# Attention feeding an expert layer: q, k and v loaded as 72 partitions, first batch cast by the DMA, x in token order

## The chip, the cores and the metric

One core of a Trainium2 chip runs the whole program. The metric is device time in microseconds (us). The engines are PE (matrix multiply; PEld is its weight load), VectorE (DVE in the profile), ScalarE (ACT), GpSimd (POOL) and SyncE (SP). DMAs are issued from SP's queue or from POOL's; those that convert fp32 to bf16 on the way are issued from POOL.

## The reference

Eight batches of eight heads; 576 tokens and a head size of 64. Keys and values are averaged over groups of eight tokens, so that 72 remain. Then comes an expert layer with h times cos(h) in the middle.

```python
k_p = k.reshape(B, H, Sp, pool, D).mean(axis=3)      # pool 8, Sp 72
v_p = v.reshape(B, H, Sp, pool, D).mean(axis=3)
scores = scale * np.matmul(q, k_p.transpose(0, 1, 3, 2))
attn = np.exp(scores); attn = attn / np.sum(attn, axis=-1, keepdims=True)
attn_out = np.matmul(attn, v_p)
x = attn_out.transpose(0, 2, 1, 3).reshape(B * S, H * D)   # 4608 x 512
h = x @ w_in                                               # 4608 x 2048
out = (h * np.cos(h)) @ w_out                              # 4608 x 512
```

## The kernel before

The 4608 tokens are nine tiles of 512. For each tile t the loop runs an **up** pass and a **down** pass. Up (`up`, L284 to L289) multiplies 64 times 128x512 on PE into three double PSUM banks in turn; ScalarE takes the cosine (a sine with a bias, L288), VectorE multiplies it with h into `g_sb` (L289). Down (`down_mm`, L292) multiplies 64 times more: four slices `ms` of 128 tokens, 16 steps each, into two single PSUM banks `obanks`. VectorE copies a finished slice to SBUF (L297) and SP stores it.

The attention of batch b = t + 1 is put between the down matmuls of tile t. The list `fill` gives to each piece of it the slot (the number of the down matmul) ahead of which it is issued; a piece that waits holds everything behind it on its engine, since the order on each engine is that of the program. In tiles 1 to 6 the pieces are the transposes of pooled k and of q at slots 2, 6 and 10, and from slot 14 every three slots one of: `scores` (two matmuls into bank 0 and an exponential on ScalarE, L211, L214), `sums` (four matmuls with ones into bank 1, a logarithm and an exponential of its negative, L221 to L225), and `values` with `normal` (four matmuls into bank 2 and a multiply on VectorE, which writes x transposed into `xT`, L234, L243). In tile 0 the pieces start at slot 36 and the attention at slot 48, one slot apart. ScalarE loads another function table for the sine and for the exponential, twice in each tile.

**Loads.** q comes cast to bf16 from POOL's queue as `q_main` (128 partitions of four tokens, 1 KB of fp32 each) and `q_rem` (the last 64 tokens, 256 bytes each). k and v are 72 partitions of eight tokens, 2 KB of fp32 per head; each load is cut into 64 and 8 partitions (`by_rows`). Batch 0's k comes uncast from SP in two halves of four heads; v of batch 0 and k, v of batch 1 come cast from POOL; k, v of batch 2 uncast from POOL, all others uncast from SP. POOL's order at the start is q of batch 0, v of batch 0, the weights, k, q, v of batch 1, k, q, v of batch 2.

**Pooling.** Batch 0's k: VectorE adds tokens 0-3 to 4-7 (L153), PE adds the remaining four and transposes in one, by matmuls with the identity (L146). Batch 0's v and batch 1's k and v: PE adds all eight by matmuls with the identity (L146, L159). From batch 2 on, POOL adds in three steps (`pool_kv`, L121 to L123).

**Order of the columns.** q's transposes (L179, L191) give the tokens of a batch as four blocks of 128 (tokens 0, 4, 8, ... first) and one of 64 (`col_of`). The columns of `xT` keep that order, and `down_out` stores rows with a stride of four.

**Start.** Batch 0's attention stands alone ahead of the loop: halves of k and q, scores of heads 0 to 3, then the other halves, then v, then rounds of `values`, `sums` and `scores`, and the first up pass.

```python
        eng.tensor_tensor(out=s[:, :, 0:4, :], in0=s[:, :, 0:4, :], in1=s[:, :, 4:8, :], op=ADD)
        eng.tensor_tensor(out=s[:, :, 0:2, :], in0=s[:, :, 0:2, :], in1=s[:, :, 2:4, :], op=ADD)
        eng.tensor_tensor(out=dst, in0=s[:, :, 0, :], in1=s[:, :, 1, :], op=ADD)
```

Of the kernel before, what the change touches and what calls it, by code (L numbers as in the profile page):

```python
# [14 lines left out]
POOL = 8  # L15
# [4 lines left out]
def kernel(  # L20
# [27 lines left out]
    kvb = ctx.enter_context(tc.tile_pool(name="kvb", bufs=3))  # L48
    kvst = ctx.enter_context(tc.tile_pool(name="kvst", bufs=2))
    qst = ctx.enter_context(tc.tile_pool(name="qst", bufs=3))  # L50
# [15 lines left out]
    def by_rows(dst, src):  # L66

        for lo, hi in ((0, 64), (64, Sp)):
            yield dst[lo:hi], src[:, lo:hi]

    def kv_view(src, b):
        return src[b].rearrange("h (p t) d -> h p (t d)", t=POOL)

    def load_kv(b, which, src, queue=nc.sync):
        st = kvst.tile([Sp, H, POOL, D], FP32, name="kv_st", tag="kv_st")
        for o, i in by_rows(st.rearrange("p h t d -> p h (t d)"), kv_view(src, b)):
            queue.dma_start(out=o, in_=i.rearrange("h p n -> p h n"))
        staged[which, b] = st

    def load_kv_cast(b, which, src):  # L80
        st = kvb.tile([Sp, H, POOL, D], BF16, name=f"{which}_b", tag="kv_b")
        for o, i in by_rows(st.rearrange("p h t d -> p h (t d)"), kv_view(src, b)):
            nc.gpsimd.dma_start(out=o, in_=i.rearrange("h p n -> p h n"))
        staged[which, b] = st

    def load_k_halves(b):
        hs = H // 2
        for j in range(2):
            st = kvst.tile([Sp, H, POOL, D], FP32, name="kv_st", tag="kv_st")[:, 0:hs]
            for o, i in by_rows(st.rearrange("p h t d -> p h (t d)"), kv_view(k, b)[j * hs:(j + 1) * hs]):  # L90
                nc.sync.dma_start(out=o, in_=i.rearrange("h p n -> p h n"))
            staged["k", b, j] = st

    def load_q(b, halves=1):
        qm = qst.tile([128, H, 4, D], BF16, name="q_main", tag="q_main")
        qr = qst.tile([64, H, D], BF16, name="q_rem", tag="q_rem")
        hs = H // halves
        for j in range(halves):
            hh = slice(j * hs, (j + 1) * hs)
            nc.gpsimd.dma_start(out=qm[:, hh].rearrange("p h t d -> p h (t d)"),  # L100
                                in_=q[b, hh, 0:512, :].rearrange("h (p t) d -> p h (t d)", t=4))
            nc.gpsimd.dma_start(out=qr[:, hh], in_=q[b, hh, 512:S, :].rearrange("h s d -> s h d"))
        pooled["q", b] = (qm, qr)
# [22 lines left out]
    def col_of(b, t):  # L126

        if b % 2 == 0:
            return 128 * t
        return 0 if t == 4 else 64 + 128 * t  # L130

    att = {}

    def heads(x, pj):
        return x[:, 2 * pj:2 * pj + 2]

    def pool_k_mm(b, bank, kb, pjs):

        if ("kpT", b) not in att:
            att["kpT", b] = asb.tile([128, KCH, Sp], BF16, name="kpT", tag="kpT")  # L140
        n, rows = len(pjs), kb.shape[2]
        ps = bank[:, 0:n * Sp].rearrange("p (j n) -> p j n", j=n)
        for i in range(n):
            for t in range(rows):
                for hp in range(2):
                    nc.tensor.matmul(ps[hp * 64:hp * 64 + 64, i, :], lhsT=kb[:, 2 * i + hp, t, :],  # L146
                                     rhs=identity[:Sp, :Sp], start=(t == 0), stop=(t == rows - 1))
        nc.vector.tensor_copy(out=att["kpT", b][:, pjs[0]:pjs[-1] + 1, :], in_=ps)

    def pool_k_half(b, j, bank):  # L150
        st = staged.pop(("k", b, j))
        kb = asb.tile([Sp, H // 2, POOL // 2, D], BF16, name="k_sum", tag="k_sum")
        nc.vector.tensor_tensor(out=kb, in0=st[:, :, 0:4, :], in1=st[:, :, 4:8, :], op=ADD)  # L153
        pool_k_mm(b, bank, kb, range(2 * j, 2 * j + 2))
# [10 lines left out]
    def q_transpose(b, bank, pjs=range(KCH)):  # L165
# [3 lines left out]
        qT = att["qT", b]  # L169
        qb, _ = pooled["q", b]  # L170
        n = len(pjs)
        if len(bank.shape) == 3:
            bank = bank.rearrange("p a n -> p (a n)")
        ps = bank.bitcast(BF16)[:, 0:n * 512].rearrange(
            "p (j t n) -> p j t n", t=4, j=n)
        for i, pj in enumerate(pjs):
            for t in range(4):
                for hp in range(2):
                    nc.tensor.matmul(ps[hp * 64:hp * 64 + 64, i, t, :], qb[:, 2 * pj + hp, t, :],  # L179
                                     identity, is_transpose=True)  # L180
        c0 = col_of(b, 0)
        nc.vector.tensor_copy(out=qT[:, pjs[0]:pjs[-1] + 1, c0:c0 + 512],  # L182
                              in_=ps.rearrange("p j t n -> p j (t n)"))

    def q_transpose_rem(b, bank, pjs=range(KCH)):
        qT = att["qT", b]
        _, qrb = pooled["q", b]
        n = len(pjs)
        ps = bank.bitcast(BF16)[:, 0:n * 64].rearrange("p (j n) -> p j n", j=n)
        for i, pj in enumerate(pjs):  # L190
            nc.tensor.matmul(ps[:, i, :], heads(qrb, pj).rearrange("p h d -> p (h d)"),  # L191
                             identity[:64, :64], is_transpose=True)
        c0 = col_of(b, 4)
        nc.vector.tensor_copy(out=qT[:, pjs[0]:pjs[-1] + 1, c0:c0 + 64], in_=ps)
# [100 lines left out]
    def down_out(t, ms, ps):  # L295
        o = msb.tile([128, d_model], FP32, name="o_sb", tag="o_sb")
        nc.vector.tensor_copy(out=o, in_=ps)  # L297
        pair, r = divmod(t * 4 + ms, 9)
        if r == 4:
            for j in range(2):  # L300
                r0 = (2 * pair + j) * S + 512
                nc.sync.dma_start(out=out[r0:r0 + 64, :], in_=o[j * 64:j * 64 + 64, :])
        else:
            b, tt = (2 * pair, r) if r < 4 else (2 * pair + 1, r - 5)
            rows = out[b * S:b * S + 512, :].rearrange("(p t) m -> t p m", t=4)
            nc.sync.dma_start(out=rows[tt], in_=o)


    load_k_halves(0)
    load_q(0, 2)  # L310
    identity = consts.tile([128, 128], BF16, name="identity")
    make_identity(nc, identity)
    ones = consts.tile([128, D], BF16, name="ones")
# [3 lines left out]

# [5 lines left out]
    load_kv_cast(1, "k", k)  # L323
    load_q(1)
    load_kv_cast(1, "v", v)
    load_kv(2, "k", k, nc.gpsimd)
    load_q(2)
    load_kv(2, "v", v, nc.gpsimd)
    exp_tables()
    pool_k_half(0, 0, obanks[0])  # L330
    q_transpose(0, banks[2], range(0, 2))
    q_transpose_rem(0, banks[2][:, 1, :], range(0, 2))
    scores(0, 0, 0, banks[0])
    scores(0, 1, 0, banks[1])
    pool_k_half(0, 1, obanks[1])
    q_transpose(0, obanks[0], range(2, 4))
    q_transpose_rem(0, obanks[1], range(2, 4))
    sums(0, 0, 0, banks[2])
    scores(0, 0, 1, banks[0])
    scores(0, 1, 1, banks[1])  # L340
    pool_v_mm(0, obanks[1])
    todo = [(0, 0), (0, 1), (1, 0), (1, 1)]
    for n, (j, sg) in enumerate(todo):
        values(0, j, sg, obanks)
        normal(0, j, sg, obanks)
        if n + 1 < 4:
            sums(0, *todo[n + 1], banks[2])
        if n + 2 < 4:
# [77 lines left out]
```

The softmax here doesn't subtract the row's maximum and nothing guards it: scores larger than these inputs give would overflow.

## Time and profile before

| what | us |
|---|---|
| median of three runs (350.87 to 352.19) | 350.93 |
| the profiled execution | 351.02 |
| its span, first to last instruction | 349.2 |
| PE busy | 326.5 |
| ACT busy | 181.6 |
| DVE busy | 154.3 |
| POOL busy | 124.4 |

The page splits the span into 40 slices of 8.73 us and gives each engine's busy share in tenths. A timeline line reads: start, duration, engine, line, operation, output <- input, partitions x elements and type, count, and in brackets the idle time before it with what ended it. A line of the chain of waits reads: start, duration, engine, tile, line; the chain is followed back from the last instruction to what released it. A line of the busy times by stretch has the stretch, its length, then for PE, PEld, DVE, ACT and POOL the busy time with the number of instructions, then the clock granted to PE, the DMA share and the GB/s that the DMAs moved.

### The profile page before, as it was taken

The page shows a single profiled execution, that of the slowest core. Times are in us where ns is not written, and L with a number is a line of the kernel's source. Part 1 is how long each engine was busy: PE and PEld are TensorE (multiplying, and loading weights), DVE is VectorE, ACT ScalarE, POOL GpSimd, SP SyncE. Part 2 cuts the span into 40 slices and gives each one's busy share as a digit, 9 for nine tenths or more (in the row PEclk, how much of TensorE's full clock was granted, in tenths as well). Part 3 has the DMA queues.
Part 4 walks back from the last instruction along what each step waited for, and adds up shares of the span by engine and source line. Part 5 has one row for each costly group of instructions (what it writes and reads, how often), then busy time and mean ns, then how long its engine had stood idle before and what let it go on. Part 6 is the DMA issues. An engine that isn't in the chain of part 4 may idle for free.

```text
span 349.2 us, 4752 instructions
## 1 busy us (share of the span) xinstructions
PE 326.5 (93%) x1960; PEld 136.4 (39%) x1960; DVE 154.3 (44%) x175; ACT 181.6 (52%) x216; POOL 124.4 (36%) x80
## 2 busy tenths in 40 slices
PE   0578999889999999999999999999999999999995
PEld 0323444334433443344334433443345334444442
DVE  1421653237523762366245723572257325723731
ACT  1146640676556655665656566565666456602600
POOL 7342317750990099008920892069100000000000
PEclk9999999999999999999999999999999999999999
DMA  9999999259518941795268617770200010012011
GB/s 140 164 204 206 189 190 224 71 64 218 96 54 138 185 80 60 116 177 107 62 98 185 118 60 99 166 137 31 60 33 0 32 60 30 2 60 60 3 54 66
DMA packets 31414, 35.77 MB, mean 102 GB/s; under 512 B 5856, under 2 KB 19872, under 8 KB 31392
## 3 DMA queue, kind: packets, MB, share of 16 engines
q0 software_dynamic: 19520, 13.05, 28.4%
q1 hardware_dynamic: 11872, 22.42, 27.5%
q8 instruction: 15, 0.25, 0.3%
q14 instruction: 7, 0.06, 0.1%
HBM read 36.70 MB, written 9.44 MB: 132 GB/s over the span
## 4 chain that ended last, share of the span: by engine, by line
PE 88%; ACT 4%; DMA 4%; DVE 1%; POOL 1%; issue 1%; ACTq 0%; POOLq 0%
PE obank L292 38%; PE bank L284 36%; PE bank L211 4%; DMA v_b<-in_v_dram 4%; PE bank L221 3%; PE bank L234 3%; PE bank L179 2%; ACT inv L225 1%; ACT lnc L223 1%; ACT ex L214 1%; PE obank L159 1%; PE bank L159 0%; POOL q_main L100 0%; PE bank L191 0%; DVE qT L182 0%
## 5 line engine op out<-in xcount | busy, mean ns | idle before, releaser
L292 PE MATMUL obank<-w_out_sb,g_sb 128*128 128x512 bf16 x576 | 148.6, 381 | 0.0
L284 PE MATMUL bank<-xT,w_in_sb 128*128 128x512 bf16 x576 | 127.6, 382 | 1.4 <-DVE xT L243 0.9
L288 ACT ACTIVATE cos<-bank,half_pi 128x1024 f32<-128x1024 f32 x72 | 80.1, 1113 | 63.8 <-PE bank L284 63.8
L289 DVE TENSOR_TENSOR g_sb<-bank,cos 128x1024 bf16<-128x1024 f32 x72 | 88.2, 1225 | 52.4 <-ACT cos L288 52.4
L121 POOL TENSOR_TENSOR kv_st<-kv_st 72x2048 f32<-72x2048 f32 x12 | 54.2, 4519 | 93.1 <-DMA kv_st<-in_k_dram 91.4
L284 PEld LDWEIGHTS <-w_in_sb 128*128 128x128 bf16 x576 | 56.6, 98 | 71.0 <-issue 4.3
L214 ACT ACTIVATE ex<-bank 72x576 bf16<-72x576 f32 x64 | 40.5, 638 | 57.1 <-PE bank L211 57.1
L292 PEld LDWEIGHTS <-g_sb 128*128 128x128 bf16 x576 | 46.8, 98 | 59.6 <-issue 12.4
L243 DVE TENSOR_TENSOR xT<-bank,inv 128x576 bf16<-128x576 f32 x28 | 21.2, 758 | 67.7 <-PE bank L234 49.3
L297 DVE COPY o_sb<-obank 128x512 f32<-128x512 f32 x36 | 24.9, 691 | 41.5 <-PE obank L292 41.0
L223 ACT ACTIVATE lnc<-bank 128x576 f32<-128x576 f32 x32 | 20.8, 650 | 28.2 <-PE bank L221 27.9
L122 POOL TENSOR_TENSOR kv_st<-kv_st 72x1024 f32<-72x1024 f32 x12 | 28.2, 2347 | 0.9
L225 ACT ACTIVATE inv<-lnc 128x576 f32<-128x576 f32 x32 | 21.9, 683 | 1.0
L211 PE MATMUL bank<-qT,kpT 64*72 64x288 bf16 x128 | 20.4, 323 | 1.5 <-ACT ex L214 1.3
L211 PEld LDWEIGHTS <-kpT 64*72 64x72 bf16 x128 | 8.0, 111 | 25.1 <-issue 25.1
L221 PE MATMUL bank<-ex,ones 72*64 72x288 bf16 x128 | 15.6, 315 | 2.0 <-ACT ex L214 1.8
L234 PE MATMUL bank<-ex,vp 72*64 72x288 bf16 x112 | 12.2, 298 | 0.0
L146 PE MATMUL obank<-identity,k_sum 72*64 72x72 bf16 x32 | 1.4, 256 | 11.4 <-DVE k_sum L153 11.4
L221 PEld LDWEIGHTS <-ones 72*64 72x64 bf16 x128 | 5.5, 113 | 14.8 <-issue 14.5
L272 ACT ACT_TABLE_LOAD x8 | 10.3, 1283 | 0.9 <-PEq L410 0.7
L182 DVE COPY qT<-bank 128x2048 bf16<-128x2048 bf16 (+1 forms) x8 | 9.2, 1150 | 2.9 <-PE bank L179 2.9
L275 ACT ACT_TABLE_LOAD x8 | 10.3, 1283 | 0.1
(44 smaller groups left out, 100.1 us busy)
## 6 DMA issues: line engine op xcount, KB each, us to landing
out_dram<-o_sb SPq DMA_DIRECT2D x32, 256.0 KB, 2.3
kv_st<-in_k_dram SPq DMA_DIRECT2D x5, 1024.0 KB, 10.8
kv_st<-in_v_dram SPq DMA_DIRECT2D x5, 1024.0 KB
q_main<-in_q_dram POOLq DMA_DIRECT2D x7, 512.0 KB, 6.6
w_in_sb<-in_moe_w_in_dram POOLq DMA_DIRECT2D x4, 512.0 KB, 16.0
w_out_sb<-in_moe_w_out_dram POOLq DMA_DIRECT2D x4, 512.0 KB, 17.7
kv_st<-in_k_dram SPq DMA_DIRECT2D x2, 512.0 KB, 5.6
v_b<-in_v_dram POOLq DMA_DIRECT2D x2, 512.0 KB, 14.7
```

What stands on the lines that cost most here:

```text
L121: eng.tensor_tensor(out=s[:, :, 0:4, :], in0=s[:, :, 0:4, :], in1=s[:, :, 4:8, :], op=ADD)
L122: eng.tensor_tensor(out=s[:, :, 0:2, :], in0=s[:, :, 0:2, :], in1=s[:, :, 2:4, :], op=ADD)
L211: nc.tensor.matmul(pair[:Sp, hp, :SEG], lhsT=kpT[hp * 64:hp * 64 + 64, pj, :], rhs=qT[hp * 64:hp * 64 + 64, pj, sg * SEG:(sg + 1) * SEG])
L214: nc.scalar.activation(out=ex, in_=pair[:Sp, :, :SEG], func=ACTF.Exp, scale=scale / POOL)
L221: nc.tensor.matmul(cs[hp * 64:hp * 64 + 64, i, :SEG], lhsT=ones[:Sp, :], rhs=ex[:, hp, :])
L223: nc.scalar.activation(out=lnc, in_=cs[:, :, :SEG], func=ACTF.Ln)
L225: nc.scalar.activation(out=inv, in_=lnc, func=ACTF.Exp, scale=-1.0)
L284: nc.tensor.matmul(h[:, j, :], lhsT=w_in_sb[fc // 4][:, ki, (fc % 4) * 128:(fc % 4 + 1) * 128], rhs=xT[:, ki, t * TILE:(t + 1) * TILE], st ...
L288: nc.scalar.activation(out=cos, in_=h, func=ACTF.Sin, bias=half_pi[:, :1])
L289: nc.vector.tensor_mul(out=g_sb[:, 2 * fp:2 * fp + 2, :], in0=h, in1=cos)
L292: nc.tensor.matmul(o, lhsT=g_sb[:, fc, ms * 128:(ms + 1) * 128], rhs=w_out_sb[fc // 4][:, fc % 4, :], start=(fc == 0), stop=(fc == FFCH - 1))
L297: nc.vector.tensor_copy(out=o, in_=ps)
```

## The change

- q, k and v are all loaded as 72 partitions with eight tokens each, 2 KB of fp32 per head. Loads from POOL's queue are no longer cut into 64 and 8 partitions; loads from SP's queue still are.
- Batch 0: k, too, comes cast from POOL, in two halves that alternate with halves of q. PE adds all eight tokens of k; VectorE's addition (`k_sum`) goes.
- q is transposed in 64 matmuls of 72 columns a batch instead of 32 of 128 and 4 of 64. The copies out of PSUM reorder the columns into token order, one copy for each pair of heads, reading with a step of 72 elements. In batch 0 VectorE and ScalarE share these copies; in tiles 0 to 6 VectorE makes all four.
- x has its columns in token order; a slice of the output is one block of 128 rows.
- Eight matmuls of 512 columns over a constant tile stand first on PE. Nothing reads their result.
- The start has another order: `sums` and `scores` of the next heads ahead of v's pooling.
- Batch 1: k and v come uncast, VectorE adds them in three steps each (slots 20 and 41 of tile 0), and batch 2's loads are issued behind these. The transposes are at slots 28, 32 and 36, the attention starts at slot 38 instead of 48.

```diff
-    kvb = ctx.enter_context(tc.tile_pool(name="kvb", bufs=3))
     kvst = ctx.enter_context(tc.tile_pool(name="kvst", bufs=2))
-    qst = ctx.enter_context(tc.tile_pool(name="qst", bufs=3))
+    qst = ctx.enter_context(tc.tile_pool(name="qst", bufs=2))
...
     def load_kv(b, which, src, queue=nc.sync):
         st = kvst.tile([Sp, H, POOL, D], FP32, name="kv_st", tag="kv_st")
-        for o, i in by_rows(st.rearrange("p h t d -> p h (t d)"), kv_view(src, b)):
-            queue.dma_start(out=o, in_=i.rearrange("h p n -> p h n"))
+
+        for lo, hi in ((0, 64), (64, Sp)) if queue is nc.sync else ((0, Sp),):
+            queue.dma_start(out=st[lo:hi].rearrange("p h t d -> p h (t d)"), in_=row_view(src, b)[lo:hi])
         staged[which, b] = st
 
-    def load_kv_cast(b, which, src):
-        st = kvb.tile([Sp, H, POOL, D], BF16, name=f"{which}_b", tag="kv_b")
-        for o, i in by_rows(st.rearrange("p h t d -> p h (t d)"), kv_view(src, b)):
-            nc.gpsimd.dma_start(out=o, in_=i.rearrange("h p n -> p h n"))
+    def row_view(src, b, h0=0, h1=None):
+        return src[b, h0:h1].rearrange("h (p t) d -> p h (t d)", t=POOL)
+
+    def load_kv_cast(b, which, src, parts=1):
+        st = kvst.tile([Sp, 2 * H, POOL, D], BF16, name="kv_st", tag="kv_st")[:, 0:H]
+        load_cast(st, b, src, parts)
         staged[which, b] = st
 
-    def load_k_halves(b):
-        hs = H // 2
...
-    def load_q(b, halves=1):
-        qm = qst.tile([128, H, 4, D], BF16, name="q_main", tag="q_main")
...
-            nc.gpsimd.dma_start(out=qm[:, hh].rearrange("p h t d -> p h (t d)"),
-                                in_=q[b, hh, 0:512, :].rearrange("h (p t) d -> p h (t d)", t=4))
-            nc.gpsimd.dma_start(out=qr[:, hh], in_=q[b, hh, 512:S, :].rearrange("h s d -> s h d"))
-        pooled["q", b] = (qm, qr)
+    def load_cast(st, b, src, parts=1, only=None):
+        hs = H // parts
+        for j in range(parts) if only is None else [only]:
+            h0, h1 = j * hs, (j + 1) * hs
+            nc.gpsimd.dma_start(out=st[:, h0:h1].rearrange("p h t d -> p h (t d)"), in_=row_view(src, b, h0, h1))
+
+    def load_q(b):
+        qb = qst.tile([Sp, H, POOL, D], BF16, name="q_b", tag="q_b")
+        load_cast(qb, b, q)
+        staged["q", b] = qb
...
+    def pool_k_mm(b, bank, pjs):
+
+        kb = staged["k", b]
         if ("kpT", b) not in att:
             att["kpT", b] = asb.tile([128, KCH, Sp], BF16, name="kpT", tag="kpT")
-        n, rows = len(pjs), kb.shape[2]
+        n, rows = len(pjs), POOL
         ps = bank[:, 0:n * Sp].rearrange("p (j n) -> p j n", j=n)
         for i in range(n):
             for t in range(rows):
                 for hp in range(2):
-                    nc.tensor.matmul(ps[hp * 64:hp * 64 + 64, i, :], lhsT=kb[:, 2 * i + hp, t, :],
+                    nc.tensor.matmul(ps[hp * 64:hp * 64 + 64, i, :], lhsT=kb[:, 2 * pjs[i] + hp, t, :],
                                      rhs=identity[:Sp, :Sp], start=(t == 0), stop=(t == rows - 1))
         nc.vector.tensor_copy(out=att["kpT", b][:, pjs[0]:pjs[-1] + 1, :], in_=ps)
...
-    def pool_k_half(b, j, bank):
-        st = staged.pop(("k", b, j))
-        kb = asb.tile([Sp, H // 2, POOL // 2, D], BF16, name="k_sum", tag="k_sum")
-        nc.vector.tensor_tensor(out=kb, in0=st[:, :, 0:4, :], in1=st[:, :, 4:8, :], op=ADD)
-        pool_k_mm(b, bank, kb, range(2 * j, 2 * j + 2))
...
+    def q_transpose(b, banks_, pjs, copies):
...
+        qT, qb = att["qT", b], staged["q", b]
+        pss = [bank.bitcast(BF16)[:, 0:S].rearrange("p (t n) -> p t n", t=POOL) for bank in banks_]
+        for ps, pj in zip(pss, pjs):
+            for t in range(POOL):
                 for hp in range(2):
-                    nc.tensor.matmul(ps[hp * 64:hp * 64 + 64, i, t, :], qb[:, 2 * pj + hp, t, :],
-                                     identity, is_transpose=True)
-        c0 = col_of(b, 0)
-        nc.vector.tensor_copy(out=qT[:, pjs[0]:pjs[-1] + 1, c0:c0 + 512],
-                              in_=ps.rearrange("p j t n -> p j (t n)"))
-
-    def q_transpose_rem(b, bank, pjs=range(KCH)):
-        qT = att["qT", b]
-        _, qrb = pooled["q", b]
-        n = len(pjs)
-        ps = bank.bitcast(BF16)[:, 0:n * 64].rearrange("p (j n) -> p j n", j=n)
-        for i, pj in enumerate(pjs):
-            nc.tensor.matmul(ps[:, i, :], heads(qrb, pj).rearrange("p h d -> p (h d)"),
-                             identity[:64, :64], is_transpose=True)
-        c0 = col_of(b, 4)
-        nc.vector.tensor_copy(out=qT[:, pjs[0]:pjs[-1] + 1, c0:c0 + 64], in_=ps)
+                    nc.tensor.matmul(ps[hp * 64:hp * 64 + 64, t, :], qb[:, 2 * pj + hp, t, :],
+                                     identity[:Sp, :Sp], is_transpose=True)
+        for ps, pj, copy in zip(pss, pjs, copies):
+            copy(out=qT[:, pj, :].rearrange("p (n t) -> p n t", t=POOL), in_=ps.rearrange("p t n -> p n t"))
 
...
-        pair, r = divmod(t * 4 + ms, 9)
-        if r == 4:
-            for j in range(2):
-                r0 = (2 * pair + j) * S + 512
-                nc.sync.dma_start(out=out[r0:r0 + 64, :], in_=o[j * 64:j * 64 + 64, :])
-        else:
-            b, tt = (2 * pair, r) if r < 4 else (2 * pair + 1, r - 5)
-            rows = out[b * S:b * S + 512, :].rearrange("(p t) m -> t p m", t=4)
-            nc.sync.dma_start(out=rows[tt], in_=o)
-
-
-    load_k_halves(0)
-    load_q(0, 2)
+        r0 = t * TILE + ms * 128
+        nc.sync.dma_start(out=out[r0:r0 + 128, :], in_=o)
+
+
+    warm = consts.tile([128, 512], BF16, name="warm")
+    nc.vector.memset(warm, 1.0)
+    exp_tables()
+    k0 = kvst.tile([Sp, 2 * H, POOL, D], BF16, name="kv_st", tag="kv_st")[:, 0:H]
+    q0 = qst.tile([Sp, H, POOL, D], BF16, name="q_b", tag="q_b")
+    staged["k", 0], staged["q", 0] = k0, q0
+    load_cast(k0, 0, k, 2, 0)
+    load_cast(q0, 0, q, 2, 0)
     identity = consts.tile([128, 128], BF16, name="identity")
     make_identity(nc, identity)
+    load_cast(k0, 0, k, 2, 1)
+    load_cast(q0, 0, q, 2, 1)
     ones = consts.tile([128, D], BF16, name="ones")
     nc.gpsimd.memset(ones, float(POOL))
     half_pi = consts.tile([128, 1], FP32, name="half_pi")
     nc.gpsimd.memset(half_pi, math.pi / 2.0)
-
     load_kv_cast(0, "v", v)
     for cg in range(4):
         load_w_in(cg)
     for cg in range(4):
         load_w_out(cg)
-    load_kv_cast(1, "k", k)
+    load_kv(1, "k", k, nc.gpsimd)
     load_q(1)
-    load_kv_cast(1, "v", v)
-    load_kv(2, "k", k, nc.gpsimd)
-    load_q(2)
-    load_kv(2, "v", v, nc.gpsimd)
-    exp_tables()
-    pool_k_half(0, 0, obanks[0])
-    q_transpose(0, banks[2], range(0, 2))
-    q_transpose_rem(0, banks[2][:, 1, :], range(0, 2))
-    scores(0, 0, 0, banks[0])
-    scores(0, 1, 0, banks[1])
-    pool_k_half(0, 1, obanks[1])
-    q_transpose(0, obanks[0], range(2, 4))
-    q_transpose_rem(0, obanks[1], range(2, 4))
-    sums(0, 0, 0, banks[2])
-    scores(0, 0, 1, banks[0])
-    scores(0, 1, 1, banks[1])
+    load_kv(1, "v", v, nc.gpsimd)
+
+    for i in range(8):
+        nc.tensor.matmul(banks[1][:, 0, :], lhsT=warm[:, 0:128], rhs=warm)
+    todo = [(0, 0), (0, 1), (1, 0), (1, 1)]
+    vec_act = (nc.vector.tensor_copy, nc.scalar.copy)
+
+    def score2(n):
+        for i in range(2):
+            scores(0, 2 * todo[n][0] + i, todo[n][1], banks[i])
+
+    def value2(n):
+        values(0, *todo[n], obanks)
+        normal(0, *todo[n], obanks)
+
+    pool_k_mm(0, obanks[0], range(0, 2))
+    q_transpose(0, [banks[2][:, 0, :], banks[2][:, 1, :]], range(0, 2), vec_act)
+    score2(0)
+    pool_k_mm(0, obanks[1], range(2, 4))
+    sums(0, *todo[0], banks[2])
+    score2(1)
+    q_transpose(0, obanks, range(2, 4), vec_act)
+    sums(0, *todo[1], banks[2])
+    score2(2)
     pool_v_mm(0, obanks[1])
-    todo = [(0, 0), (0, 1), (1, 0), (1, 1)]
-    for n, (j, sg) in enumerate(todo):
-        values(0, j, sg, obanks)
-        normal(0, j, sg, obanks)
-        if n + 1 < 4:
-            sums(0, *todo[n + 1], banks[2])
-        if n + 2 < 4:
-            for i in range(2):
-                scores(0, 2 * todo[n + 2][0] + i, todo[n + 2][1], banks[i])
+    value2(0)
+    sums(0, *todo[2], banks[2])
+    value2(1)
+    score2(3)
+    value2(2)
+    sums(0, *todo[3], banks[2])
+    value2(3)
     sin_tables()
 
     for t in range(NT):
@@ -358,17 +322,20 @@
         mms = [(ms, fc) for ms in range(4) for fc in range(FFCH)]
         fill = []
         if more:
+            vec2 = (nc.vector.tensor_copy,) * 2
+            early = [lambda: k_transpose(b, banks[2][:, 0, :]),
+                     lambda: q_transpose(b, [banks[0][:, i, :] for i in range(2)], range(0, 2), vec2),
+                     lambda: q_transpose(b, [banks[1][:, i, :] for i in range(2)], range(2, 4), vec2)]
+            at, first, gap = [2, 6, 10], 14, 3
             if t == 0:
-                early = [lambda: pool_k_mm(b, banks[0][:, 0, :], staged["k", b], range(KCH)),
-                         lambda: q_transpose(b, banks[1]),
-                         lambda: q_transpose_rem(b, banks[0][:, 1, :]),
-                         lambda: pool_v_mm(b, banks[2][:, 0, :])]
-                at, first, gap = [36, 44, 46, 50], 48, 1
-            else:
-                early = [lambda: k_transpose(b, banks[2][:, 0, :]),
-                         lambda: q_transpose(b, banks[0]),
-                         lambda: q_transpose_rem(b, banks[2][:, 1, :])]
-                at, first, gap = [2, 6, 10], 14, 3
+                def pool_first(which, src):
+                    pool_kv(b, which, nc.vector)
+                    load_kv(b + 1, which, src, nc.gpsimd)
+                    if which == "k":
+                        load_q(b + 1)
+                early.insert(0, lambda: pool_first("k", k))
+                early.append(lambda: pool_first("v", v))
+                at, first, gap = [20, 28, 32, 36, 41], 38, 1
             fill = list(zip(at, early))
             fill += [(first + gap * i, f) for i, f in enumerate(att_main(b))]
             fill.sort(key=lambda x: x[0])
```

## The prediction

> **What bounds the kernel now.** I read the page first (parts 1, 2 and 4), then the chain in order of time, then the timelines of the start, of the first tile and of a later tile, and last the DMA figures by stretch. The page:
>
> ```profile
> span 349.2 us, 4752 instructions
> PE 326.5 (93%) x1960; PEld 136.4 (39%) x1960; DVE 154.3 (44%) x175; ACT 181.6 (52%) x216; POOL 124.4 (36%) x80
> PE   0578999889999999999999999999999999999995
> ```
>
> PE carries the span except in the first three slices (26 us) and near 60 us. From tile 1 on a tile takes 35.9 us (74.92 to 110.54 to 146.43 us in the chain), and none of that waits for VectorE, ScalarE or a DMA. The change must win or lose at the start and in tile 0. The chain of waits at the start:
>
> ```profile
> 4.88 0.61 POOL v_b L83
> 5.50 12.68 DMA v_b<-in_v_dram
> 18.31 3.61 PE obank L159 x8
> 21.94 0.70 DVE vp L162
> ...
> 30.71 0.69 ACT inv L225
> 31.43 0.47 DVE xT L241
> 31.94 14.63 PE bank L284 x62
> ```
>
> The load of v bounds the start: v lands at 18.3 us, eight matmuls pool it, and then sums, logarithm and exponential alternate between PE and ACT until the last x is written at 31.43 + 0.41 = 31.84 us. The timeline there:
>
> ```profile
> 7.22 1.22 DVE L153 TENSOR_TENSOR k_sum<-kv_st 72x1024 bf16<-72x1024 f32 x1 [7.22 <-DMA kv_st<-in_k_dram]
> 8.74 0.74 POOL L106 DMA_DIRECT2D w_in_sb<-in_moe_w_in_dram  x1 [1.11 <-DMA q_main<-in_q_dram]
> 10.79 0.15 PEld L191 LDWEIGHTS <-q_rem 64*128 64x128 bf16 x2 [0.99 <-DMA q_rem<-in_q_dram]
> ...
> 16.10 0.69 DVE L182 COPY qT<-obank 128x1024 bf16<-128x1024 bf16 x1 [0.55 <-PE obank L179]
> ```
>
> First halves of k and q land at 7.22, 8.74 and 10.79 us; the scores start at 10.84. And the DMA by stretch (last column GB/s):
>
> ```profile
> 24.00:28.00 4.00, 3.11 (x20) 1.18 (x17) 0.89 (x3) 3.33 (x6) 0.98 (x2) 1.00 1.24 207
> 28.00:32.00 4.00, 2.56 (x13) 0.88 (x11) 1.40 (x4) 3.35 (x6) 1.28 (x2) 1.00 1.24 206
> 48.00:52.00 4.00, 4.00 (x20) 1.78 (x19) 1.67 (x2) 1.02 (x1) 0.00 (x0) 1.00 1.10 193
> ```
>
> GB/s counts what is written: the casting weight loads (28 us) write 206, the load of k of batch 2, uncast (48 us), 193. Per second about as many bytes land either way, so a cast halves a load's time.
>
> Tile 0's end in the chain, and in tile 1's timeline the place where q's transposes meet the scores:
>
> ```profile
> 72.72 0.66 ACT lnc L223
> 73.40 0.69 ACT inv L225
> 74.11 0.77 DVE xT L243
> 74.92 13.54 PE bank L284 x62
> ```
>
> ```profile
> 91.01 1.22 DVE L182 COPY qT<-bank 128x2048 bf16<-128x2048 bf16 x1
> ...
> 93.00 0.31 PE L211 MATMUL bank<-qT,kpT 64*72 64x288 bf16 x2
> ```
>
> In tile 0 the attention of batch 1 outlasts the down matmuls, and PE waits for the last x; in tile 1 q's main copy ends 0.8 us before the first score.
>
> [...] L182 moves 1024 bf16 in 0.69 us. The new copy reads PSUM with step 72, which no row shows. [...] No row shows a 72-partition load; today they are cut into 64 + 8. [...] the 512-column matmul is spaced 0.43 us at 31.94 us and 0.216 in later tiles (64 in 13.81).
>
> **Start.** Loads: now k (1.18 MB as fp32), q and v (0.59 each as bf16) write 2.36 MB before v is in; after, 1.77 MB, with no 128-byte rows of q_rem. All are on POOL. The first POOL load issues at 1.25 us and has 288 rows (L102's 256 take 0.62); SP's k issues at 0.74 and the first stretch with traffic begins at 2, so I take 1.25 + 0.65 + 1.5, first bytes at 3.5 (an estimate). [...] the five loads come to the same 9.6 us (1.77 MB at 206 GB/s is 8.6[...]). From last byte to waiter I take 1.5 us (half of k now: 0.59 MB from about 2.3 us at 200 GB/s is in at 5.3, its waiter starts at 7.22). The arrivals are then k 7.0, q 8.6, k 10.2, q 11.8, v 15.0. POOL waits on nothing here; identity is ready at about 3.4.
>
> Compute, with PE cold as today: 32 pooling matmuls 0.86 (twice the 0.43 of 16, L146), 32 transposes of 72 columns 0.96[...], four score, sum or value matmuls 0.6, 0.6, 0.5 (L211, L221, L234 spacing), two exponentials 1.16, ln + inverse 1.36 (L223, L225), v 3.45 and 0.69 for its copy. [...] ACT's is taken as its 576-element row, 0.67. So: transposes 8.6 to 9.6, copies to 10.4, scores and exponentials to 11.8; sums, ln, inverse to 13.7; second exponentials to 14.9; ACT copy of q to 15.5; scores; v 15.9 to 19.35, vp 20.2 (v is no longer waited for); value 0 to 21.65; last scores' exponentials 24.0; last sums, ln 25.1, inverse 25.8; last x 26.3. The same working with today's order and arrivals ends at 31.70, trace 31.84; so I take 26.4: **-5.4 us**. A later first load moves this one for one; below, k cannot arrive before about 6 (-1 us more). The eight idle matmuls (8 x 0.43) sit in the wait for k: nothing. They end at 4.5 and PE is idle until 7.0, so I expect the clock to have fallen back.
>
> **Tile 0** (times from its first down matmul; now the next up pass starts in full at 74.92 - 46.41 = 28.5, two of its matmuls already done). Now: k pooling on PE 1.16, v 1.73, score at 13.5, then four rounds of about 3.05 us set by ACT (two exponentials, ln, inverse). After: DVE adds of k cost 2.29 + 1.22 + 0.69 = 4.2 us[...] and start behind the copy of slice 0, 4.35, ending 8.55. The key transpose stands at slot 28, PE time 6.1: **PE waits 2.4 us**, with everything of PE behind it. Then q transposes, four copies to 13.5, then v's adds 13.5 to 17.7, for which the first value product waits 1.5 us more. Scores start at 12.3 instead of 13.5, and the rounds run on to x at 27.2, while ten down matmuls, which now stand behind the rounds, end at 28.0. With today's order this working gives 27.5 for PE and 28.8 for x (trace 28.46), so 0.35 long: after, the next pass starts at 27.65 against 28.5 less 0.43 for the two matmuls done: **-0.4 us**; bounds -2 and +2 (an add one third faster or slower). k of batch 1 has the same bytes ahead as now (7.14 MB) and lands about 41 against 46 needed; v about 50 against 55: hidden, but cover is 5 us. Batch 2's loads start only after these adds, yet k2's POOL adds end near tile time 27 against the 42 needed, v2's near 35 against 51.
>
> **Tiles 1 to 6.** PE: 64 transposes at 0.018 (the 64 of L146 take 1.16) against 32 + 4 in 1.01 + 0.22: -0.07 each, -0.4 together. DVE: four copies 3.0 us instead of 1.22 + 0.29. In tile 1 they start at 91.01; bank 0 is free at 92.45, the score comes at 92.93: hidden with 0.45 us to spare. Bounds per copy: 0.67, and 1.36[...]. SP queue unchanged; out stores become whole blocks of the same bytes, nothing.
>
> Sum: 351.02 - 5.4 - 0.4 - 0.4 = 344.8, rounded to **345.0**; the profiled run is 0.09 above the median of 350.93, too little to shift.
>
> **Rivals.**
> A, loads later (first bytes at 4.7 as q's now[...], so +3): 347.5 to 350. For: all hangs on POOL now, and today's q issued at 1.25 lands only at 8.74. Against: k's packets lay ahead of it.
> B, slow strided copies: at 1.36 us bank 0 is free at 93.65, a stall of 0.75 in six tiles (4.5), in tile 0 +2.4, at the start +0.5: 352.4, slower than before; it decides from about 1.3 us a copy, where the three stalls eat the 6.2 gained. For: step 72 was never timed. Against: DVE takes f32 from PSUM[...] (L243, 576 in 0.76).
> C, few engines: 72 partitions on eight, at half rate. v lands at 22.2 (start +0.9 against now), k of batch 1 at 54 and v at 71, eight us after it is needed: about 359. For: loads are cut into 64 + 8 today. [...]
> D, the idle matmuls do keep the clock up: v's pooling 1.7 less, the up pass 1.2 less: 342.
>
> **How the numbers follow.** Forecast (343.2 to 347.2) 0.46; A 0.16, C 0.19, B 0.14, D 0.05. What can be told from no change is 0.5%, 1.75 us. Faster: 0.46 + 0.05 + 0.10 of A = 0.61; same: 0.06 of A + 0.05 of B = 0.11; slower: 0.09 of B + C = 0.28. Range 342.5 to 355: forecast, A, B and the near end of C.
>
> **What would show it.** Right: v of batch 0 landing near 15 and not on the chain, first full up pass near 26.4, two PE waits on DVE in tile 0 (2.4 and 1.5), copies of 0.76, later tiles of 35.8. Wrong: k of batch 0 later than 9, a PE wait on DVE's qT copies in tiles 1 to 6, v of batch 1 later than 55, a cadence of 0.216 already in v's pooling.

## The result, and the profile after

The changed kernel takes 354.59 us (median of 4 runs, 354.09 to 356.68) against 350.98 us (4 runs, 350.87 to 352.19) for the kernel before in the same comparison: ratio 1.0106 with a 95% interval of 1.0058 to 1.0154. The forecast was 345.0 us: 1.7% faster was expected, and 1% slower came. Laid out by stage, from the two profiled executions (us; "tile 0" runs from its first down matmul to the start of the next up pass; in the kernel before two matmuls of that pass are done by then, which moves 0.4 us of its forecast to the next row):

| stage | before | after | forecast |
|---|---|---|---|
| up to the first down matmul | 46.41 | 41.12 | 41.0 |
| tile 0 | 28.5 | 36.4 | 27.65 |
| from there to the end of the span | 274.3 | 274.7 | 274.3 |
| span | 349.2 | 352.2 | 343.0 |

Where executions of one kernel lie more than 1.5% apart, only its fastest are compared, which leaves two of the experiments below without a ratio. The start won what it was to win, and tile 0 lost 8 us. The page of the changed kernel, span, TensorE's busy tenths and the granted clock in 40 slices of 8.8 us each:

```profile
span 352.2 us, 5105 instructions
...
PE   5889964899999999999999999999999999999995
...
PEclk9558998569999999999999999999999999999999
```

The sixth and seventh slices (44 to 62 us) are a hole in TensorE's work, and the clock row has two dips: slices two and three, and slices seven to nine (53 to 79 us), where it goes down to half (0.50 of full speed from 60 to 76 us). The chain of waits there:

```profile
24.18 33.94 DMA kv_st<-in_v_dram
58.21 2.30 DVE kv_st L107
60.53 1.23 DVE kv_st L108
74.22 3.44 PE obank L250 x10
77.66 8.42 PE bank L242 x39
```

The chain enters tile 0 through the load of v of batch 1, issued at 24.18 us and in at 58.12. VectorE's timeline (start, duration, line, tile, shapes; in brackets what it waited for):

```profile
45.57 2.29 DVE L107 TENSOR_TENSOR kv_st<-kv_st 72x2048 f32<-72x2048 f32 x1
47.89 1.22 DVE L108 TENSOR_TENSOR kv_st<-kv_st 72x1024 f32<-72x1024 f32 x1
49.14 0.69 DVE L109 TENSOR_TENSOR kp<-kv_st 72x512 bf16<-72x512 f32 x1
...
53.35 1.42 DVE L152 COPY qT<-bank 128x576 bf16<-128x576 bf16 x2 [0.19 <-PE bank L149]
58.21 2.29 DVE L107 TENSOR_TENSOR kv_st<-kv_st 72x2048 f32<-72x2048 f32 x1 [3.44 <-DMA kv_st<-in_v_dram]
60.53 1.22 DVE L108 TENSOR_TENSOR kv_st<-kv_st 72x1024 f32<-72x1024 f32 x1
61.79 0.69 DVE L109 TENSOR_TENSOR vp<-kv_st 72x512 bf16<-72x512 f32 x1
```

In the names, kp and vp are the pooled k and v of batch 1, and the first matmuls with vp are its first value product. The additions have exactly the durations that the author estimated (2.29, 1.22 and 0.69 us). Those of v stand 3.44 us still for their data. And TensorE's timeline of the same stretch, cut to the lines that decide:

```profile
49.89 0.30 PE L159 MATMUL bank<-identity,kp 72*128 72x72 bf16 x4 [2.56 <-DVE kp L109]
...
57.38 0.39 PE L250 MATMUL obank<-w_out_sb,g_sb 128*128 128x512 bf16 x1
62.53 0.69 PE L192 MATMUL bank<-ex,vp 72*64 72x288 bf16 x4 [4.76 <-DVE vp L109]
63.15 0.61 PE L250 MATMUL obank<-w_out_sb,g_sb 128*128 128x512 bf16 x1
...
74.22 3.44 PE L250 MATMUL obank<-w_out_sb,g_sb 128*128 128x512 bf16 x10 [0.33 <-issue]
```

Both waits stand where the forecast put them, the second far longer. Compare the single down matmul L250 ahead of the second wait and behind it: 0.39 and 0.61 us. The same work takes longer afterwards, because the clock was halved meanwhile. A stall on another engine was paid twice: as the wait, and as slower work behind it. From the first value product to the next up pass it took 77.50 - 62.53 = 15.0 us.

### The profile page after: what moved, and what is told of

It is laid out like the page before. It is cut to its first block, busy times and chain, and to the rows that moved or that the text cites. A ratio compares the mean times of both kernels' runs of the same rounds, so it can differ in the third digit from the quotient of the medians.

```text
span 352.2 us, 5105 instructions
## 1 busy us (share of the span) xinstructions
PE 329.2 (93%) x2119; PEld 137.8 (39%) x2156; DVE 169.1 (48%) x191; ACT 182.7 (52%) x218; POOL 116.8 (33%) x68
## 3 DMA queue, kind: packets, MB, share of 16 engines
q0 software_dynamic: 13696, 14.82, 26.9%
## 4 chain that ended last, share of the span: by engine, by line
PE 83%; DMA 11%; DVE 2%; issue 2%; ACT 1%; POOL 0%; DVEq 0%; POOLq 0%
PE obank L250 36%; PE bank L242 31%; DMA kv_st<-in_v_dram 10%; PE bank L169 4%; PE bank L179 3%; PE bank L192 3%; PE bank L149 2%; DMA q_b<-in_q_dram 2%; PE obank L134 1%; DVE kv_st L107 1%; PE obank L192 1%; DVE kv_st L108 0%; ACT ex L172 0%; PE obank L127 0%; PE bank L159 0%
## 5 line engine op out<-in xcount | busy, mean ns | idle before, releaser
L250 PE MATMUL obank<-w_out_sb,g_sb 128*128 128x512 bf16 x552 | 146.9, 387 | 2.7 <-issue 2.4
L242 PE MATMUL bank<-xT,w_in_sb 128*128 128x512 bf16 x563 | 125.8, 381 | 1.5 <-DVE xT L199 0.6
L250 PEld LDWEIGHTS <-g_sb 128*128 128x128 bf16 x576 | 47.1, 98 | 62.1 <-issue 16.8
L181 ACT ACTIVATE lnc<-bank 128x576 f32<-128x576 f32 x32 | 20.8, 650 | 25.2 <-PE bank L179 25.1
L152 DVE COPY qT<-bank 128x576 bf16<-128x576 bf16 x29 | 20.1, 749 | 2.2 <-PE bank L149 2.2
L192 PE MATMUL bank<-ex,vp 72*64 72x288 bf16 x112 | 13.2, 319 | 4.8 <-DVE vp L109 4.8
L149 PEld LDWEIGHTS <-q_b 72*64 72x64 bf16 x512 | 10.3, 117 | 8.0 <-issue 5.9
L192 PEld LDWEIGHTS <-vp 72*64 72x64 bf16 x128 | 5.3, 116 | 19.1 <-issue 12.1
L149 PE MATMUL bank<-identity,q_b 72*64 72x72 bf16 x480 | 11.0, 202 | 1.2 <-DMA q_b<-in_q_dram 1.2
```

Source lines behind the costliest of these rows:

```text
L149: nc.tensor.matmul(ps[hp * 64:hp * 64 + 64, t, :], qb[:, 2 * pj + hp, t, :], identity[:Sp, :Sp], is_transpose=True)
L192: nc.tensor.matmul(ao[i][hp * 64:hp * 64 + 64, :SEG], lhsT=vp[:, 2 * pj + hp, :], rhs=ex[:, hp, :])
L242: nc.tensor.matmul(h[:, j, :], lhsT=w_in_sb[fc // 4][:, ki, (fc % 4) * 128:(fc % 4 + 1) * 128], rhs=xT[:, ki, t * TILE:(t + 1) * TILE], st ...
L250: nc.tensor.matmul(o, lhsT=g_sb[:, fc, ms * 128:(ms + 1) * 128], rhs=w_out_sb[fc // 4][:, fc % 4, :], start=(fc == 0), stop=(fc == FFCH - 1))
```

## The experiments

Theory after the result: VectorE's additions of batch 1 hold TensorE up twice, the clock falls in the waits, and the rest of tile 0 runs at half speed. Rivals: the late load of v alone ("late data"); the waits alone, whatever the clock; the idle matmuls at the start. Every ratio is to the kernel before on the same chip, whose medians were 351.15 us (e1 to e4), 351.75 (e5 to e8), 351.65 (e9 to e11) and 351.6 (e12).

**Loads cut as before (e1).** The 72 partitions of GpSimd's uncast loads go out as 64 + 8.

```diff
-        for lo, hi in ((0, 64), (64, Sp)) if queue is nc.sync else ((0, Sp),):
+        for lo, hi in ((0, 64), (64, Sp)):
```

> The changed kernel, but POOL's uncast loads (k and v of batches 1 and 2) are cut into 64 and 8 partitions again. Load theory (72 whole partitions move at 146 to 164 GB/s in the stretch from 36 to 48 us, where 64 + 8 moved 185 to 195): v of batch 1 lands near 54 us instead of 58.2, VectorE waits for it less than 1 us instead of 3.4, PE's wait for v's sums falls from 4.8 to about 2 us and its clock is not halved afterwards; time 346 to 347.5. Rival, volume (uncast loads write twice the bytes, the cut is no matter): v lands at 57 to 58, time as the changed kernel, 354. Rival, VectorE's adds themselves: time 352 to 354 whatever the landing.

Measured: 353.54 us (352.32 to 354.8, 5 runs), ratio 1.0062 (1.0032 to 1.0091). The cut hardly moved the load: v of batch 1 came in at 57.2 us instead of 58.1 (the load theory said 54). VectorE doesn't wait for it here, but only because VectorE itself was free later, at 58.19 instead of 54.77 us: tile 0 began 2.1 us later in this execution, and the query transposes ran partly at half clock. TensorE's two waits have about the forecast lengths:

```profile
51.83 0.30 PE L159 MATMUL bank<-identity,kp 72*128 72x72 bf16 x4 [2.37 <-DVE kp L109]
...
62.49 0.69 PE L192 MATMUL bank<-ex,vp 72*64 72x288 bf16 x4 [1.23 <-DVE vp L109]
```

Yet the clock is halved (0.50) from 52.2 to 55.6 and from 62.5 to 76.1 us, and tile 0 takes 34.05. The load theory's 346 to 347.5 fell.

**Idle matmuls (whose result nothing reads) in the second wait alone (e2), and none at the start (e4).**

```diff
+                def idle():
+                    for _ in range(20):
+                        nc.tensor.matmul(banks[2][:, 0, :], lhsT=warm[:, 0:128], rhs=warm)
+                fill.insert([i for i, x in enumerate(fill) if x[0] == 43][0], (43, idle))
```

> The changed kernel with 20 idle matmuls of 512 columns (20 x 0.216 = 4.3 us) ahead of the first value product of tile 0, in PE's wait for v's sums. Nothing lands earlier. Clock theory (the 4.8 us wait lets PE's clock fall to half from 59.4 to 76.5 us, which costs 4.9 of the 8.3 us that tile 0 lost): no half-clock stretch there, tile 0 ends about 5 us earlier, time 349 to 350. If the halved clock costs nothing because ScalarE sets the rounds of attention anyway: no change, 354 to 355.

Measured: 352.39 us (351.66 to 353.37, 6 runs), ratio 1.0039 (1.002 to 1.0059). The clock now fell at the first wait (2.43 us for kp): query transposes took 1.17 us a set instead of 0.71. The filler ran 62.04 to 66.45 us, though vp was ready at 63.2, and so gave back 3.3 us of what the full clock behind it won (first value product to up pass 10.1 us instead of 15.0). This run filled one wait of two and too much of it; it decides little, and the 349 to 350 us of the clock theory weren't reached.

```diff
-    for i in range(8):
-        nc.tensor.matmul(banks[1][:, 0, :], lhsT=warm[:, 0:128], rhs=warm)
```

> The changed kernel without the eight idle matmuls at the start. Prediction's step (they do nothing, the clock has fallen back by the time k lands): time within 1 us of the changed kernel, start of the first full up pass unchanged at 26.9 us. Rival (they bring the clock up earlier in the first up pass, which was at full speed after 1.8 us against 2.2 before): up to 1.5 us slower.

Measured: 353.52 us (349.57 to 355.95, 12 runs), ratio 1.003 (0.9996 to 1.0064). The idle matmuls aren't the cause. The wide spread goes with the clock: the three executions of 349.6 us have a mean granted clock of 0.99, those of 353.4 to 353.7 us one of 0.976. In the profiled one (354.51) it fell at the first wait (2.71 us) and stayed down to the end of tile 0 (36.5 us). What decides how much an execution loses isn't shown.

**Pooling of batch 1 back on TensorE (e3).** k and v of batch 1 are cast and pooled by matmuls at the same slots, nothing of it on VectorE, and batch 2's loads are issued at the start, as in the kernel before; the rest of the change stays.

```diff
-                early.insert(0, lambda: pool_first("k", k))
-                early.append(lambda: pool_first("v", v))
-                at, first, gap = [20, 28, 32, 36, 41], 38, 1
+                early[0] = lambda: pool_k_mm(b, banks[2][:, 0, :], range(KCH))
+                early.append(lambda: pool_v_mm(b, banks[2][:, 1, :]))
+                at, first, gap = [28, 32, 36, 41], 38, 1
```

> The changed kernel, but batch 1's k and v come cast and PE adds them by matmuls with the identity as before the change (slots 28 and 41), with buffers of their own, and batch 2's loads are issued at the start. Start, q's transposes and token order stay. Load theory and VectorE theory: PE waits for VectorE in tile 0 go away, the start keeps its 5 us, time 344 to 346.5. If the tile 0 loss came from the new slots or from q's copies: 351 or more.

Measured: 346.3 us (345.41 to 347.04, 4 runs), ratio 0.9862 (0.9836 to 0.9888): faster than both kernels. Tile 0 takes 27.3 us, no wait for VectorE, clock full (1.00) throughout it. So the loss lies in how batch 1 is loaded and added, all of it; the rest of the change is worth 4.9 us here.

**Both waits filled (e5), the first wait covered by work (e6).** e5 leaves loads and additions as they are and only keeps TensorE running.

```diff
+                fill.insert([i for i, x in enumerate(fill) if x[0] == 28][0], (28, lambda: idle(12, banks[2][:, 1, :])))
+                fill.insert([i for i, x in enumerate(fill) if x[0] == 43][0], (43, lambda: idle(16, banks[2][:, 0, :])))
```

> Idle matmuls stand in both of TensorE's waits of tile 0: 12 of 512 columns (2.6 us at full clock) before the key transpose, 16 (3.4 us) before the first value product. Clock theory (the waits themselves are short; what they cost is the halved clock after each): no half-clock stretch in tile 0 or only a short one, single down matmuls stay at 0.22 to 0.4 us, q transposes 0.64 us a set, tile 0 from its first down matmul to the next up pass 29 to 32 us instead of 36.4, whole kernel 347 to 350 us. Rival (the additions on VectorE and the late v alone bound tile 0, whatever the clock): tile 0 stays at 33.5 us or more and the kernel at 352 to 354.

Measured: 349.19 us (348.93 to 349.76, 4 runs), ratio 0.9932 (0.9907 to 0.9956). Its TensorE timeline (L344 is the idle matmul):

```profile
48.86 2.75 PE L344 MATMUL bank<-warm 128*128 128x512 bf16 x11
...
59.15 3.62 PE L344 MATMUL bank<-warm 128*128 128x512 bf16 x16
62.70 0.44 PE L192 MATMUL bank<-ex,vp 72*64 72x288 bf16 x4
63.07 0.39 PE L250 MATMUL obank<-w_out_sb,g_sb 128*128 128x512 bf16 x1
...
72.81 7.50 PE L242 MATMUL bank<-xT,w_in_sb 128*128 128x512 bf16 x33
```

The first value product comes at 62.70 us, as in the changed kernel (62.53), but from there to the up pass it takes 10.1 us instead of 15.0, L250 again 0.39. Tile 0 takes 30.0 us, 6.4 less: 4.9 of it behind the value product, and 1.5 because tile 0 began 1.7 us later in this execution (42.81 us), while v came in at 57.3. Work that computes nothing, put into the waits, made the kernel 5 us faster. This is the clock's share, shown; the rival of waits alone falls.

```diff
-                at, first, gap = [20, 28, 32, 36, 41], 38, 1
+                at, first, gap = [20, 38, 42, 46, 51], 48, 1
```

> The key transpose and all behind it stand 10 down matmuls later in tile 0 (slots 38, 42, 46, 51, first score at 48), so that 2.2 us of needed work takes the place of the first wait. Clock theory: the wait for kp falls under 1 us and the clock holds through the query transposes; the wait for vp stays, at 3 to 5 us, and halves the clock after it, with fewer matmuls left to stretch: tile 0 32 to 35 us, kernel 350 to 353. Rival (the first wait costs only its own 2.5 us and the end is set by vp): tile 0 unchanged within 0.7 us, kernel 353.5 to 355.

Measured: 350.58 us (349.21 to 355.37, 20 runs), ratio 0.9966 (0.995 to 0.9982). The wait for kp is 0.56 us, that for vp 2.83; the clock still halved behind the second (59.5 to about 76 us), where fewer matmuls were left. The time is as expected of the clock theory; tile 0, at 31.3 us, lies a little below its 32 to 35, and the next up pass began at half clock.

**Shorter additions and fewer bytes (e7), fewer bytes alone (e10, e12).** In e7 batch 1 is cast in the DMA and VectorE adds in bf16.

```diff
-    load_kv(1, "k", k, nc.gpsimd)
+    load_kv_cast(1, "k", k)
     load_q(1)
-    load_kv(1, "v", v, nc.gpsimd)
+    load_kv_cast(1, "v", v)
```

> k and v of the second batch are cast to bf16 in the DMA, so half as many bytes are written, and VectorE adds in bf16. If lateness of the data is the cause: k lands near 43 instead of 45.5 and v before 50, VectorE waits for neither, and with 4.2 us of additions as before the wait for kp is about 2.4 us and that for vp under 2: kernel 350 to 352. If the additions also get shorter (each below 1.5 us instead of 2.29), both waits go under 1 us, the clock stays up, and the kernel takes 345 to 347.5, the predicted 345.0 within its tile 0. [...]

Measured: 344.25 us (343.83 to 344.97, 4 runs), ratio 0.9791 (0.9765 to 0.9817). VectorE's timeline, and TensorE's:

```profile
47.63 1.21 DVE L107 TENSOR_TENSOR kv_st<-kv_st 72x2048 bf16<-72x2048 bf16 x1
48.87 0.69 DVE L108 TENSOR_TENSOR kv_st<-kv_st 72x1024 bf16<-72x1024 bf16 x1
49.60 0.42 DVE L109 TENSOR_TENSOR kp<-kv_st 72x512 bf16<-72x512 bf16 x1
```

```profile
50.08 0.30 PE L159 MATMUL bank<-identity,kp 72*128 72x72 bf16 x4 [0.50 <-DVE kp L109]
...
57.88 0.44 PE L192 MATMUL bank<-ex,vp 72*64 72x288 bf16 x4
...
68.49 11.82 PE L242 MATMUL bank<-xT,w_in_sb 128*128 128x512 bf16 x53
```

Three additions take 2.3 us instead of 4.2, no data is late, the wait for vp is gone, and tile 0 takes 25.1 us, less than before (28.5). e10 takes this apart: the loads stay cast, the sums are kept in fp32.

```diff
+        if b == 1:
+            s = asb.tile([Sp, H, 4, D], FP32, name="sum4", tag="sum4", bufs=1)
-        eng.tensor_tensor(out=s[:, :, 0:4, :], in0=s[:, :, 0:4, :], in1=s[:, :, 4:8, :], op=ADD)
+        eng.tensor_tensor(out=s[:, :, 0:4, :], in0=s0[:, :, 0:4, :], in1=s0[:, :, 4:8, :], op=ADD)
```

> Second batch cast in the DMA as in the run that took 344.25 us, but the sums of four and of two tokens kept in fp32, so that half the bytes are written and the additions should take near the 4.2 us of the changed kernel again (2.29, 1.22, 0.69). Theory 'length of the additions': TensorE waits 2 to 2.7 us for kp and 0.5 to 2 for vp though no data is late, the clock halves in some executions: 346.5 to 351 us, with a wide spread. Theory 'late data': VectorE waits for no data, so the time is that of the bf16 additions, 344.3 within 0.8 us.

Measured: 350.46, 356.99, 358.73 and 359.2 us. The profiled execution is that of 358.73 us; it shows a stall of its own (last section), so nothing is drawn from its time. e12 was to keep GpSimd's additions away from VectorE's by loading batch 2 later:

```diff
-                    load_kv(b + 1, which, src, nc.gpsimd)
-                    if which == "k":
-                        load_q(b + 1)
+                    if which == "v":
+                        load_kv(b + 1, "k", k, nc.gpsimd)
+                        load_q(b + 1)
+                        load_kv(b + 1, which, src, nc.gpsimd)
```

> Batch 1 cast in the DMA and its sums kept in fp32, as before, but batch 2 is loaded only once both of batch 1 are added, so that GpSimd's own additions can't run beside VectorE's. Theory 'length of the additions': VectorE waits for no data, its six additions take 2.28, 1.22 and 0.69 us twice, TensorE waits 2.4 us for kp and 1 to 3 us for vp[...]: 347 to 351.5 us. Theory 'late data': 344.3 to 345 us. If the 4.9-us addition of the run before is VectorE's own doing and not GpSimd's, it comes again and the time is above 355.

Measured: 350.59, 351.51, 357.64 and 358.35 us. The edit moved nothing: GpSimd's issue of the load of k waited for VectorE's first addition of k alone (over at 48.04 us) and came at 48.33 us still, which makes this in effect the same kernel as e10. But its profiled execution (350.59) is free of the stall, and so is a clean reading of long additions without late data:

```profile
50.07 0.30 PE L162 MATMUL bank<-identity,kp 72*128 72x72 bf16 x4 [2.37 <-DVE kp L112]
...
59.18 0.44 PE L195 MATMUL bank<-ex,vp 72*64 72x288 bf16 x4 [1.23 <-DVE vp L112]
...
60.25 0.61 PE L253 MATMUL obank<-w_out_sb,g_sb 128*128 128x512 bf16 x1
...
74.12 11.17 PE L245 MATMUL bank<-xT,w_in_sb 128*128 128x512 bf16 x50
```

VectorE waits for no data here, TensorE waits 2.37 and 1.23 us, the clock halves at 59.9 us, and from first value product to up pass it takes 14.9 us. Tile 0: 36.4 in the changed kernel, 32.6 with early data (v came in at 46.8 us), 25.1 with early data and short additions. One execution each, but the three differ by far more than steady tiles do.

**The fast versions without idle matmuls (e8, e9), and with later slots (e11).** e8 is e3, e9 is e7, each without the eight idle matmuls at the start (the edit of e4); e11 is e9 with

```diff
-                at, first, gap = [20, 28, 32, 36, 41], 38, 1
+                at, first, gap = [20, 34, 38, 42, 46], 44, 1
```

> Second batch cast and pooled on TensorE as in the run before that took 346.3 us, and the eight idle matmuls at the start left out. If they do nothing by the time the first batch's work begins, as predicted: 346.3 within 0.7 us, first up pass at the same place within 0.3 us. If they keep the clock up for part of the first batch: 0.5 to 2 us slower, and the first up pass as much later.

> Second batch cast and added in bf16 on VectorE, and the eight idle matmuls at the start left out. If the idle matmuls give nothing: 343.5 to 344.5 us. If they warm the first batch's work: 0.5 to 2 us more than 344.25.

> As the bf16 additions without idle matmuls, with the key transpose and all behind it 5 to 6 down matmuls later (slots 34, 38, 42, 46, first score at 44), so that needed work stands where TensorE waited 1.0 us for kp. If that wait is all that is left: 342.8 to 343.8 us. If the attention at the end of tile 0 then has too few down matmuls between ScalarE's exponentials: no gain, or up to 1 us more.

Measured: e8 346.09 us (345.99 to 346.28, 4 runs) against 346.3; e9 343.89 (343.56 to 344.42, 4 runs; ratio 0.9789, 0.9761 to 0.9817) against 344.25; e11 344.61 (342.82 to 345.21, 4 runs). The idle matmuls do nothing that can be measured. e11's tile 0 is 24.45 us instead of 25.12; but its first down matmul comes at 44.03 us instead of 42.01, in a part that the edit doesn't touch, where TensorE waited 1.07 us for v of batch 0 (over all runs it comes between 41.1 and 44.0), so a gain of 0.7 isn't shown in the time. e9 is the fastest version found, together with e7.

Tile 0 in one table (us; "clock" is that behind the first value product, half 0.50 and full 1.00, "to up" the time from that product to the next up pass):

| run | wait for kp | wait for vp | clock | to up | tile 0 |
|---|---|---|---|---|---|
| after | 2.56 | 4.76 | half | 15.0 | 36.4 |
| e1, cut loads | 2.37 | 1.23 | half | 14.8 | 34.05 |
| e4, no idle matmuls | 2.71 | 0 | half | 15.1 | 36.5 |
| e5, both waits filled | filled | filled | full | 10.1 | 30.0 |
| e12, early data | 2.37 | 1.23 | half | 14.9 | 32.6 |
| e7, early data, bf16 | 0.50 | 0 | full | 10.6 | 25.1 |
| e3, on TensorE | 0 | 0 | full | 10.6 | 27.3 |

## Why the prediction was wrong

It was wrong by 9.6 us, and nearly all of it in one step, **tile 0**.

- **Start, -5.4: right, in part by luck.** The first full up pass begins at 26.86 us (forecast 26.4), and v of batch 0 is not waited for. k was in at 6.05, before the forecast 7.0, but v only at 16.2 instead of 15.0, just as TensorE came to it. In the twelve experiments, whose edits leave batch 0's loads alone, v came in between 15.9 and 17.7 us, TensorE waited 0.17 to 1.16 us for it in six of them, and the pass began between 26.9 and 28.3.
- **Tile 0, the waits.** The step said "PE waits 2.4 us" and 1.5 us at the first value product. The first measured 2.56. The second measured 4.76, because v of batch 1, "about 50 against 55: hidden, but cover is 5 us", landed at 58.1. The cover was gone by 3.44 us. The term that was mis-sized is the loads' rate: q and v, 1.77 MB, were given 9 us behind k, 197 GB/s, between the 206 of the weight loads (128 partitions) and the 193 of k of batch 2 (64 + 8). k, too, came in at 45.5 instead of 41, just as VectorE was free for it. The DMA by stretch of the changed kernel (last column GB/s) shows the weights in the first line and mainly k and q of batch 1, 72 partitions, in the others:

```profile
28.00:32.00 4.00, 4.00 (x18) 1.76 (x17) 1.22 (x1) 2.15 (x2) 0.00 (x0) 0.91 1.24 206
...
40.00:44.00 4.00, 4.00 (x20) 1.83 (x19) 2.69 (x3) 3.11 (x3) 0.00 (x0) 1.00 1.22 146
44.00:48.00 4.00, 3.33 (x16) 1.30 (x14) 3.09 (x3) 0.00 (x0) 0.00 (x0) 1.00 1.24 159
```

  From 4 to 10 us, when mainly batch 0's loads of 72 partitions ran, it was 141 to 156 too, where the working had taken 206 and a margin. Cutting k and v into 64 + 8 (e1) didn't bring it back (132 to 134 GB/s at 40 to 48 us), so why it is lower stays open. From 50.13 us on the load of k of batch 2 ran beside that of v; what part of the delay is its doing, no run separates.
- **Tile 0, what follows the waits.** This is the part that was missing altogether. The step let the last rounds run from 17.7 to 27.65 in tile time, 10 us, at full clock; they took 15.0. The half clock, which the forecast read from up matmuls 0.43 us apart at the start and 0.216 in later tiles, was applied to the start alone. With 21.4 - 17.7 = 3.7 us for the later first value product and 5.0 for the halved clock, the 8.7 us by which tile 0 (36.4) missed 27.65 are accounted for. The experiments show each part: in e12 v is early and the waits are those of the forecast (2.37 and 1.23 against 2.4 and 1.5), and tile 0 still takes 32.6, 5.0 above 27.65; e5 takes 4.9 away by keeping the clock up (15.0 to 10.1 us).
- **Tiles 1 to 6, -0.4: not there.** From the up pass of tile 2 to that of tile 7 a tile takes 35.94 us (113.59 to 293.31 us, five tiles), before 35.9. The copies took 0.75 us (the author's estimate was 0.76) and were hidden, as said; the saving of 0.07 a tile wasn't.
- **Idle matmuls, nothing: right** (e8, e9).
- **Rivals.** C had the right place, a late v of batch 1 in tile 0, for a rate of half; it was about three quarters (146 to 159 GB/s from 40 to 48 us, 206 for the weights). None of them had the clock in tile 0; D looked for it at the start only.

How long a wait has to be to bring the clock down, the runs don't show. In e12 it fell 0.7 us after a wait of 1.23 us, in the midst of small matmuls, while the wait of 2.37 us ahead of it, behind dense matmuls, left it up. In e1 a wait of the same length at the same place brought it down, so length alone doesn't decide. In the changed kernel it was half for 20.5 us (8.2 to 28.7) and for 17.1 us (59.4 to 76.5); what sets these lengths isn't shown.

## What to carry to other kernels

Waits of TensorE couldn't be priced at their length here: with waits of 1.23 us (e1, e12) to 4.76 us (the changed kernel) ahead of it, the work from first value product to up pass took 15 us instead of 10 at half clock. Ask what runs behind a wait and whether it is dense enough to bring the clock back: here ten down matmuls in a row did (from 74.22 us, full at 76.5), the rounds ahead of them (64 to 72 us) didn't. As an estimate from 10 and 15 us, add half of the sparse work that follows. Where work is moved from a busy engine to an idle one, its latency on the new engine must fit between its data and its consumer; 4.2 us of fp32 additions did not, 2.3 us in bf16 did. And a load's landing is better forecast from the rate at which loads like it ran (here 141 to 156 GB/s from 4 to 10 us) than from bytes at the best rate seen (206).

## What the hardware showed that was not expected

**The attention rounds kept the clock up but didn't bring it back.** In e7 the attention rounds of tile 0 run at full clock (1.00) with gaps of up to 0.48 us. In the changed kernel the same rounds at half clock, TensorE busy in all of 64 to 72 us, stayed at half (0.50) for over 11 us, and in e4 transposes and rounds together for 27 us (49.9 to 77.2); the clock came back only in the run of dense down matmuls from 74.22 us on (at 76.5), and in e12 in that from 70.40 us on (at 73.5). This isn't a rule for all lighter work: in e1 and e2 the clock was back at 55.6 and 57.9 us, among query transposes and groups of four down matmuls.

**An addition of VectorE took 4.91 us beside one of GpSimd.** In the profiled execution of e10 one addition took seven times its usual 0.69 us. VectorE's timeline, then GpSimd's:

```profile
61.26 4.91 DVE L112 TENSOR_TENSOR vp<-sum 72x512 bf16<-72x512 f32 x1
```

```profile
61.10 4.51 POOL L110 TENSOR_TENSOR kv_st<-kv_st 72x2048 f32<-72x2048 f32 x1
```

GpSimd's addition began 0.16 us earlier, and VectorE's ended 0.6 us after it. That the one held the other up is the author's estimate from these times. In e12's profiled execution GpSimd began at 59.01 us, when VectorE's last addition (58.44 to 59.13) was already running, and it took its 0.69 us. That this is what sets the executions of 357 to 359 us apart wasn't shown; only one was profiled.

**The clock row has a blind spot at the front.** In e9 it reads full (1.00 from 20 to 28 us) from the first slice on, while four value matmuls take 0.69 us at 23.24 us and 0.44 at 56.52: there the matmuls' own spacing told the clock, not the row.
